# Both layers' weights of a chunk prepared together, sum buffers in 4 KB pieces, and three copies per pair, in a banded attention and FFN kernel

## The chip, the cores and the metric

One core of a Trainium2 chip. The metric is the device time of one execution in microseconds; a lower time is better. TensorE (PE) does matrix products, PEld is its weight load, VectorE is DVE, ScalarE is ACT, GpSimd is POOL, and SyncE (SP) issues the transfers (DMAs).

## The reference

```python
# q, k, v: (8, 8, 576, 64) float32;  w_in: (512, 2048), w_out: (2048, 512) float64
scores = q @ k.T / sqrt(64)                       # per batch and head
mask   = (rel >= 0) & (rel < 64)                  # rel = query position - key position
attn   = softmax(where(mask, scores, -1e9))
x      = (attn @ v) as 4608 tokens x 512
h      = x @ w_in
g      = where(h >= 1, h, where(h <= -1, 0, (h + 1)**2 / 4))
out    = g @ w_out                                # float32
```

## The kernel before

The 4608 tokens are nine tiles of 512. Each tile needs its attention (36 steps of 128 tokens in all) and then both FFN layers, taken in 16 chunks of 128 hidden features: chunk f has first-layer weights `wts[f, 0]` (L873 multiplies by them) and second-layer weights `wts[f, 1]` (L924). Weights and activations are each split into a high and a low part of float32r, and three products are summed.

**Weights.** They arrive as 64-bit floats and are turned into the two parts once, during tile 0: a load (`w_load`, L284), two ACT passes (`w_rest` L317, `w_sign` L294), three short DVE passes (L298, L298, L310), `w_join` (L321), `w_high` (ACT, L265) and `w_low` (DVE, L333). The first four chunks are done singly, layer by layer. From chunk 4 on the work is done in doubles: one double is one layer of the two chunks f and f+1, so the first layers of 4 and 5 come in one double and their second layers in another.

**Two ways of computing the first layer.** Tiles 0 and 1 (t < PLAIN) compute it plainly. Tiles 2 to 8 use a scheme with seven products per pair of chunks instead of eight (`ffn_products`, L824; the sums of the products are put together in `h` by L840). For it the kernel forms, during tile 1, for each of the eight pairs n of chunks, the seven operands of weights and keeps them in DRAM (`kept[n]`):
- `sum_pass` (L723) copies the three operands that are plain weights. Before, these are six copies per pair: three operands, for the high and the low part each.
- `sum_whole`, `sum_sums`, `sum_high`, `sum_low` (L734, L743, L265, L753) compute the four others on DVE, POOL and ACT in a buffer `half`, for the two halves c of a pair, and `sum_keep` (L758, L759) stores them. A pair's second half c=1 follows the first. For n < 2 the buffers are those of tile 0's activations (`xh0`, `xl0`), so that n=1 needs what n=0 has stored; later they lie in `TMP_SLOT` and `H_SLOT`.

During tiles 2 to 8, `ring_load` (L796) reads the kept operands of a pair back into two rings of two slots each. The rings, the tile's operands (`x_tiles`; `xs` in the trace) and `h` lie in space that held first-layer weights, which is free once tile 1 and the sums have used it.

**The order of the work** is written by a planner (`Plan`): each piece of work has a key, a cost per engine, pieces it comes after, and buffers it takes and gives back. The planner goes through planned time engine by engine, takes the piece with the lowest key among those that can start, and writes it down. What it writes is the program order of each engine and of SP's queue, and every engine works in that order. Its costs decide the order and nothing else: a piece that in truth takes longer than planned holds up what stands behind it. A DMA's planned cost is SP's time, plus a lag until what needs it can go on. Keys count steps; a tile of 512 tokens is 21.33 steps, so a chunk is 4/3 steps. The sums have the key `step(1) + S_PACE * n + S_LATE`.

The dependences between instructions are by region of a buffer, and waits are set for them whatever the planner assumes.

A gate (L897) is the step min/max that ends a chunk's activation; it frees the PSUM buffer `ps_h`, of which there are two.

Of the kernel before, what the change touches and what calls it, by code (L numbers as in the profile page):

```python
# [20 lines left out]
P = 128  # L21
# [19 lines left out]
W_LEAD = 0.57  # L41
W_PAIR = 0, 2.0
W_FIRST = (20.54, -1.96, 1.46, 0.57, -0.16)
# [7 lines left out]
W0_KEY = -100.2  # L51
FIRST_LOAD = 0, 1, 0
M_LATE = 1
W0_STEP = 11.75
FINE = 4
# [31 lines left out]
PLAIN = 2  # L87
S_LATE = 2
S_LATER = 2
S_PACE = 2  # L90
# [5 lines left out]
EARLY_2 = 1.5  # L96
IN_A = "w6_0", "w8_0"
IN_B = "w10_0", "w12_0"
H_SLOT = "w4_0"
TMP_SLOT = "w3_0"  # L100
# [93 lines left out]
def banded_attention_then_ffn(ctx: ExitStack, tc: tile.TileContext, q, k, v, w, masks, out, dims):  # L194
# [3 lines left out]
    NP = H // 2  # L198
    NF = 2 * w.shape[0]
    NB = S // QB  # L200
# [78 lines left out]
    def w_load(g, eng=nc.sync):  # L279
        f, nf, u = g  # L280
        m = nf * DM
        ws[g] = t = wpool.tile([P, 4 * m], U16, name="raw", tag=f"w{f}_{u}")
        src = w[f // 2, :, u, f % 2:f % 2 + nf].bitcast(U16)
        eng.dma_start(out=t[:, :4 * m - 1], in_=src.rearrange("p f n -> p (f n)")[:, 1:])  # L284

    def w_sign(g):

        m = g[1] * DM  # L290
# [21 lines left out]
    def w_rest(g):  # L312

        m = g[1] * DM
# [8 lines left out]
    def w_high(g, eng):  # L323
        f, nf, u = g
        ws[g] = t = wpool.tile([P, nf, 2, DM], F32R, name="wts", tag=f"w{f}_{u}")
        for j in range(nf):
            wts[f + j, u] = t[:, j]
        us[g] = us[g].bitcast(F32).rearrange("p (u n) -> p u n", n=DM)
        copy(eng, t[:, :, 0], us[g])
# [6 lines left out]

    def add_weights(f, nf, unit):
        g = f, nf, unit
        m = nf * DM
        act, high, join, low, small = 105 + .916 * m, 92 + .844 * m, 10 + 1.22 * m, 67 + 1.05 * m, 90 + .25 * m  # L340
        key = f * W_STEP - (W_FIRST[f] if f < len(W_FIRST) else W_LEAD) + (W_PAIR[unit] if nf == 2 else .5 * unit)
        x = add(W0_KEY + W0_STEP * (f + .5 * nf * unit), dict(SP=W_LOAD * nf), lambda e: None if g == FIRST_LOAD else w_load(g), lag=DMA_LAG)
# [8 lines left out]
        for j in range(nf):  # L351
            w_ready[f + j, unit] = x

# [144 lines left out]


    xfs, xops = {}, {}  # L500

# [6 lines left out]
    def x_tiles(t):  # L508
        if t in xops:
            return  # L510
        shape = [P, 2, 2, 2, 2 * SB]
        a, b = (xpool.tile(shape, F32R, name="xs", tag=f"{n}{t % 2}") for n in ("xh", "xl"))
        if t % 2:
            c = wpool.tile(shape, F32R, name="xs", tag="w14_0")
            rest = [c[:, 0], c[:, 1], wpool.tile(shape[:1] + shape[2:], F32R, name="xs", tag="w3_0")]
        else:
            rest = [wpool.tile(shape[:1] + shape[2:], F32R, name="xs", tag=f"w{f}_0") for f in range(3)]
        xops[t] = a, b, rest, [rest[0], a[:, 1], b[:, 0], a[:, 0], rest[1], b[:, 1], rest[2]]
# [200 lines left out]
    def sum_pass(n):  # L719
        f0, f1 = by_chunk(n)  # L720
        for part in range(2):
            for o, w_, e in (0, f0, 0), (5, f0, 1), (6, f1, 1):
                nc.sync.dma_start(out=kept[n][:, part, :, o], in_=w_[:, part, :, e].bitcast(F32))  # L723

    def sum_whole(n, c, i, eng):
        if i:
            pass
        elif n < 2:
            half_of[n, c] = [xpool.tile([P, 8, P], F32, name="half", tag=("xh0", "xl0")[c])]
        else:  # L730
            half_of[n, c] = [wpool.tile([P, 8, P], F32, name="half", tag=H_SLOT if n > 2 and c else TMP_SLOT)]
        t = half_of[n, c][0]
        w_ = by_chunk(n)[i]
        engine[eng].tensor_tensor(  # L734
            out=t[:, 2 * i:2 * i + 2], in0=w_[:, 0, c].bitcast(F32), in1=w_[:, 1, c].bitcast(F32), op=ALU.add
        )
# [26 lines left out]
    def add_sums(n):  # L763
        key = step(1) + S_PACE * n + (S_LATE if n < 2 else S_LATER)
        ready = [w_ready[2 * n, 0], w_ready[2 * n + 1, 0]]
        xp = add(key, dict(SP=1600), lambda e: sum_pass(n), ready + [x_in[0]], lag=DMA_LAG)
        reads, keeps = [xp], [xp]
        for c in range(2):
            after = ready + ([x_in[0]] if n < 2 else [l1[1, 3], *sums_read[1]]) + sum_last
            if n == 2 and c:  # L770
                after.append(keeps[-1])
            elif n == 3 and not c:
                after.append(sums_kept[2][-1])
            elif n > 2 and c:
                after += [l1[1, 4], l1[1, 5], *sums_read[2]]
            k = key + c * S_PACE / 2
# [8 lines left out]
            x = add(k, tt(4 * P), lambda e, c=c: sum_low(n, c, e), [xh], shared=True)  # L785
            x = add(k, dict(SP=1500), lambda e, c=c: sum_keep(n, c), [x], lag=DMA_LAG, gives=[("tmp", xs), ("o", xh)])
            keeps.append(x)
# [5 lines left out]
    def ring_load(t, n, i):  # L793
        rings[t, n, i] = r = wpool.tile([P, 2, 2, 4 - i, P], F32R, name="wr", tag=(IN_A, IN_B)[i][n % 2])
        for part in range(2):
            nc.sync.dma_start(out=r[:, part].bitcast(F32), in_=kept[n][:, part, :, R_OPS[i]])  # L796

    ring_last = [[], []]

    def add_ring(t, n, i, key):  # L800
        after = [*sums_kept[n], *ring_last[i]]
        if t == PLAIN and n < 2:
            m = int((IN_A, IN_B)[i][n % 2].split("_")[0][1:]) // 2
# [7 lines left out]
    prods, hs, hbox = {}, {}, []  # L811

    def ffn_products(t, n, i):
# [7 lines left out]
        for ps, c, o, k in todo:  # L821
            for j, (part, xp) in enumerate(((0, 0), (0, 1), (1, 0))):
                for cp in range(2):
                    nc.tensor.matmul(  # L824
                        ps[:, c * 2 * SB:(c + 1) * 2 * SB], lhsT=r[:, part, cp, o], rhs=xo[k][:, xp, cp],
                        start=i < 2 and c == 0 and j == 0 and cp == 0,
                        stop=(i == 2 or i == 3 and c == 1) and j == 2 and cp == 1, skip_group_check=True,
                    )

    def h_of(t, n):  # L830
        if not hbox:
            hbox.append(wpool.tile([P, 2, 4 * 2 * SB], F32, name="h", tag=H_SLOT))
        return hbox[0][:, n % 2]

# [151 lines left out]
    def add_ffn(t):  # L986
        first, before, x_out = {}, [x_in[t - 1]] if t else [], {}
        done, gates = None, []
        for q in range(NF):
            f = place(t, q)  # L990
            for r, key in parts(t, q):
# [36 lines left out]
                for i0 in subs(r) if by_sub else [None]:  # L1028
                    some = subs(r) if i0 is None else [i0]
                    xo = add(  # L1030
                        key + out_late(t, q, i0), dict(PE=3 * len(some) * 229), lambda e, f=f, r=r, i0=i0: ffn_out(t, f, r, i0),
                        [xl, w_ready[f, 1], *over], takes=[] if q else ["acc"] * len(some),
# [34 lines left out]
    for f in range(NF):  # L1067
        for unit in range(2):
            if f < FINE:
                add_weights(f, 1, unit)  # L1070
            elif f % 2 == 0:
                add_weights(f, 2, unit)
    for t in range(len(TILES)):
# [4 lines left out]
        if t + 1 == PLAIN:  # L1078
            for n in range(NF // 2):
                add_sums(n)  # L1080
            x_after[t + 1] = [l1[1, f] for f in range(3)] + sums_read[0] + sums_read[1] + sums_kept[0] + sums_kept[1]
            x_after[t + 2] = [l1[1, NF - 1], *sums_read[7], *sums_kept[7]]
# [59 lines left out]
```

## Time and profile before

| | |
|---|---|
| median of 3 runs | 906.59 us (905.62 to 907.96) |
| the profiled execution's own time | 907.99 us |
| its span, first to last instruction | 906.2 us |
| mean granted TensorE clock | 0.987 |
| SP's transfers of operands to DRAM | 48 plain copies of 128 KB, 32 stores of 256 KB |
| weight loads | 8 of 511.8 KB, 12 of 1023.8 KB |

The page gives busy shares by engine, then the span in 40 slices of 22.7 us, each digit a tenth of busy time (9 is 90% or more); the row of the granted clock has tenths of full speed. An answer for a stretch of time has the stretch, its length, then for each engine the busy us and the count of instructions, then the clock, the busy share of the 16 DMA engines and GB/s. In the order of time, a row has start and length in us, and in brackets the idle time ahead and what ended it. Tile 1's first products come at about 132.7 us, tile 2's at 254.8 us.

### The profile page before, as it was taken

The numbers are of one execution on the slowest core, as the hardware profiler recorded it, in microseconds if no ns is written. First come the engines' busy times: TensorE is split into PE (matmuls) and PEld (weight loads), VectorE is DVE, ScalarE is ACT, GpSimd is POOL, SyncE is SP. The second block draws the span as 40 slices with busy tenths as digits, with TensorE's granted clock in tenths as the row PEclk, the third lists the DMA queues.
The fourth block names the chain that finished last, engine by engine and source line by source line (L and its number), as shares of the span: only waits on it lengthen the run. The fifth ranks groups of instructions, "written<-read, shape, count | busy, mean of one in ns | idle before, by whom it ended". The sixth has DMA issues, their size and how long they took to land.

```text
span 906.2 us, 20363 instructions
## 1 busy us (share of the span) xinstructions
PE 875.5 (97%) x7839; PEld 762.9 (84%) x7839; DVE 656.1 (72%) x1391; ACT 506.8 (56%) x1291; POOL 264.2 (29%) x268
## 2 busy tenths in 40 slices
PE   7699997999799999999999999999999999999998
PEld 5587885887688888888898889888988888899997
DVE  6999996598977868777686767676767676833331
ACT  7998863554455555655565537454655565434343
POOL 1000034455432232423142324232413242322222
PEclk9999996999899999999999999999999999999999
DMA  9991149447567666766676658666765664557531
GB/s 333 410 377 55 54 146 291 146 157 239 198 214 226 213 199 215 253 204 193 218 251 216 216 181 285 204 204 216 260 208 194 206 228 163 164 169 237 175 117 47
DMA packets 108033, 187.60 MB, mean 207 GB/s; under 512 B 8480, under 2 KB 49696, under 8 KB 107936
## 3 DMA queue, kind: packets, MB, share of 16 engines
q1 hardware_dynamic: 107648, 185.38, 60.9%
q8 instruction: 62, 1.02, 0.5%
q10 hardware_dynamic: 288, 0.92, 0.3%
q14 instruction: 35, 0.29, 0.1%
HBM read 162.15 MB, written 24.12 MB: 206 GB/s over the span
## 4 chain that ended last, share of the span: by engine, by line
PE 75%; DVE 12%; DMA 5%; ACT 3%; issue 2%; SPq 2%; POOL 0%; ACTq 0%; DVEq 0%
PE acc L924 36%; PE ps_h L824 27%; PE ps_h L873 6%; DVE ptd L455 4%; PE ps_a L484 3%; PE ps_a L409 3%; DVE a L897 2%; DMA kept<-half 2%; DMA kt<-in_k 2%; SPq L723 1%; ACT a L885 1%; DVE h L840 1%; DVE sm L449 1%; DVE half L734 1%; DVE half L743 1%
## 5 line engine op out<-in xcount | busy, mean ns | idle before, releaser
L924 PE MATMUL acc<-wts,gh 128*128 128x512 f32 x1154 | 363.2, 396 | 2.7 <-ACT o L265 2.7
L824 PEld LDWEIGHTS ps_h<-xs,wr 128*128 128x128 f32 x2352 | 294.5, 189 | 10.3 <-DVE h L840 0.7
L824 PE MATMUL ps_h<-xs,wr 128*128 128x256 f32 x2352 | 299.2, 282 | 0.3 <-DVE h L840 0.3
L907 POOL TENSOR_TENSOR gl<-a,gh 128x512 fp32r<-128x512 f32 (+1 forms) x130 | 167.6, 1290 | 427.5 <-ACT gh L902 389.7
L924 PEld LDWEIGHTS acc<-wts,gh 128*128 128x128 f32 x1154 | 207.9, 189 | 44.6 <-ACT o L265 3.4
L924 PE MATMUL acc<-wts,gl 128*128 128x512 f32 x577 | 225.9, 391 | 0.0
L840 DVE TENSOR_TENSOR h<-h,ps_h 128x256 f32<-128x256 f32 x280 | 117.5, 420 | 127.8 <-PE ps_h L824 113.0
L902 ACT CAST gh<-a 128x512 fp32r<-128x512 f32 (+1 forms) x149 | 90.0, 604 | 133.9 <-PE acc L924 112.2
L455 DVE STREAM_TRANSPOSE ptd<-sm 32x256 f32<-32x256 f32 x336 | 146.5, 436 | 6.3
L924 PEld LDWEIGHTS acc<-wts,gl 128*128 128x128 f32 x577 | 108.7, 188 | 23.9
L885 ACT ACTIVATE a<-h 128x512 f32<-128x512 f32 x112 | 69.9, 624 | 72.3 <-DVE h L840 71.4
L897 DVE SCALAR_TENSOR_TENSOR a<-a,h 128x512 f32<-128x512 f32 x112 | 85.7, 765 | 27.7 <-ACT a L890 16.2
L873 PE MATMUL ps_h<-xh,wts 128*128 128x512 f32 (+1 forms) x296 | 93.3, 385 | 10.7 <-DVE a L897 6.6
L437 ACT ACTIVATE sm<-sm,nm 128x96 f32<-128x96 f32 (+1 forms) x256 | 93.0, 365 | 12.2 <-DVE nm L430 12.1
L890 ACT ACTIVATE a<-a 128x512 f32<-128x512 f32 (+1 forms) x139 | 85.8, 617 | 4.3
L873 PEld LDWEIGHTS ps_h<-xh,wts 128*128 128x128 f32 x296 | 56.8, 200 | 22.6 <-DVE a L897 8.1
L873 PE MATMUL ps_h<-xl,wts 128*128 128x512 f32 (+1 forms) x148 | 56.3, 380 | 0.7 <-DVE xl L497 0.6
L265 ACT COPY h<-ps_h 128x256 f32<-128x256 f32 x77 | 28.7, 372 | 47.3 <-PE ps_h L824 43.6
L549 POOL TENSOR_TENSOR xs<-u,xs 128x256 fp32r<-128x256 f32 (+1 forms) x45 | 42.3, 971 | 32.0 <-ACT xs L265 32.0
L734 POOL TENSOR_TENSOR half<-wts 128x256 f32<-128x256 f32 x12 | 9.4, 790 | 140.1 <-PE ps_h L873 123.7
L437 ACT ACTIVATION_READ_ACCUMULATOR sm<-sm,nm 128x1 f32 x256 | 47.9, 187 | 0.0
L484 PEld LDWEIGHTS ps_a<-ptd,vt 128*64 128x64 f32 x992 | 32.0, 137 | 13.1 <-DVE ptd L455 3.6
(89 smaller groups left out, 728.3 us busy)
## 6 DMA issues: line engine op xcount, KB each, us to landing
wr<-kept SPq DMA_DIRECT2D x112, 512.0 KB, 4.7
wr<-kept SPq DMA_DIRECT2D x112, 384.0 KB, 3.9
vt<-in_v SPq DMA_DIRECT2D x72, 256.0 KB, 4.9
kt<-in_k SPq DMA_DIRECT2D x35, 384.0 KB, 5.4
raw<-in_w SPq DMA_DIRECT2D x12, 1023.8 KB, 10.3
qt<-in_q SPq DMA_DIRECT2D x36, 256.0 KB, 4.8
out<-o SPq DMA_DIRECT2D x33, 256.0 KB, 4.0
kept<-wts SPq DMA_DIRECT2D x48, 128.0 KB, 2.4
```

The costliest lines, as they stand in the source:

```text
L437: nc.scalar.activation(sm[:, p, :], (ps if masked else sm)[:, p, :], AF.Exp, bias=nm[:, p:p + 1], scale=scale if masked else 1.0, accum_ou ...
L455: nc.vector.transpose(dst[:, :, r], src[:, :, c * SQ:(c + 1) * SQ])
L484: nc.tensor.matmul(ps[half[h], p, n], lhsT=vt[i][:, c:c + D], rhs=pt[h][:, p, n], start=True, stop=True)
L824: nc.tensor.matmul(ps[:, c * 2 * SB:(c + 1) * 2 * SB], lhsT=r[:, part, cp, o], rhs=xo[k][:, xp, cp], start=i < 2 and c == 0 and j == 0 and ...
L840: nc.vector.tensor_tensor(out=h[:, to:to + 256], in0=h[:, of:of + 256], in1=ps[:, at:at + 256], op=ALU.add)
L873: nc.tensor.matmul(ps, lhsT=wts[f, 0][:, part, c * P:(c + 1) * P], rhs=x[:, c, r], start=(c == 0 and j == 0), stop=(c == NP - 1 and j == 2),)
L885: nc.scalar.activation(gs[t, f, r.start][0], phs[t, f, r.start], AF.Relu, bias=0.5, scale=0.5)
L890: nc.scalar.activation(a, a, AF.Square)
L897: nc.vector.scalar_tensor_tensor(out=a, in0=a, scalar=1.0, in1=ps, op0=ALU.min, op1=ALU.max)
L902: nc.scalar.copy(g[1], g[0])
L907: engine[eng].tensor_tensor(out=g[2], in0=g[0], in1=g[1].bitcast(F32), op=ALU.subtract)
L924: nc.tensor.matmul(acc[t, i][:, n], lhsT=g[:, sub], rhs=wts[f, 1][:, part, n], start=(q == 0 and j == 0), stop=(q == NF - 1 and j == 2 and ...
```

## The change

1. **Weights.** From chunk 4 on a double is both layers of one chunk (`add_weights(f, (0, 1))`); the host lays the weights out to match, and the size and number of the loads stay. Keys: a double of chunk f has the key of the first layer of chunk f; before, the second layers of a pair came two steps after the first ones.
2. **Pieces.** The second-layer weights of a chunk now stand beside the first-layer weights in one 8 KB buffer, so the space that becomes free is the 4 KB half `piece(f)`. Operands of even tiles lie in the pieces of chunks 4, 5 and 2 (before: 0, 1, 2), of odd ones in 14, 15 and `TMP_SLOT`; the rings in pieces 6 to 13; `h` in the buffers of chunks 0 and 1 (before: 4 and 5), and with it the second halves of the later sums. The lists of what has to be over by then are changed to match.
3. **Copies.** `sum_pass` makes three copies per pair in place of six, each for both parts at once.
4. **Gates.** In tiles 0 and 1 a gate is no longer planned after the gate before it.
5. **Planner figures.** A pass costs SP 2000 ns in place of 1600, a store 750 in place of 1500; both have a lag of 2300 ns in place of 1300; the sums' keys are one step higher (S_LATE, S_LATER 2 to 3); a second-layer product of tiles 0 and 1 is planned at 232 ns in place of 229.

```diff
-FIRST_LOAD = 0, 1, 0
+FIRST_LOAD = 0, (0,)
-S_LATE = 2
-S_LATER = 2
+S_LATE = 3
+S_LATER = 3
-IN_A = "w6_0", "w8_0"
-IN_B = "w10_0", "w12_0"
-H_SLOT = "w4_0"
+X_PIECES = (4, 5, 2), (14, 15)
+R_PIECES = (6, 8), (10, 12)
+H_SLOT = "w0_0", "w1_0"
...
-    def add_weights(f, nf, unit):
-        g = f, nf, unit
-        m = nf * DM
+    def add_weights(f, units):
+        g = f, units
+        m = len(units) * DM
...
-        key = f * W_STEP - (...) + (W_PAIR[unit] if nf == 2 else .5 * unit)
+        key = f * W_STEP - (...) + .5 * units[0]
...
+    def piece(f):
+        return wts[f, 0].rearrange("p a n -> p (a n)")
...
     def sum_pass(n):
         f0, f1 = by_chunk(n)
-        for part in range(2):
-            for o, w_, e in (0, f0, 0), (5, f0, 1), (6, f1, 1):
-                nc.sync.dma_start(out=kept[n][:, part, :, o], in_=w_[:, part, :, e].bitcast(F32))
+        for o, w_, e in (0, f0, 0), (5, f0, 1), (6, f1, 1):
+            nc.sync.dma_start(
+                out=kept[n][:, :, :, o].rearrange("p a c n -> p (a c) n"),
+                in_=w_[:, :, :, e].bitcast(F32).rearrange("p a c n -> p (a c) n"),
+            )
...
-        xp = add(key, dict(SP=1600), lambda e: sum_pass(n), ready + [x_in[0]], lag=DMA_LAG)
+        xp = add(key, dict(SP=2000), lambda e: sum_pass(n), ready + [x_in[0]], lag=O_LAG_DMA)
...
-                after += [l1[1, 4], l1[1, 5], *sums_read[2]]
+                after += [l1[1, 0], *sums_read[0]]
...
-            x = add(k, dict(SP=1500), lambda e, c=c: sum_keep(n, c), [x], lag=DMA_LAG, ...)
+            x = add(k, dict(SP=750), lambda e, c=c: sum_keep(n, c), [x], lag=O_LAG_DMA, ...)
...
-            needs += [l1[1, 4], l1[1, 5], *sums_kept[NF // 2 - 1]]
+            needs += [l1[1, 0], l1[1, 1], *sums_read[0], *sums_kept[NF // 2 - 1]]
...
-                gates = [xg]
+                gates = [xg] if t >= PLAIN else []
...
-    for f in range(NF):
-        for unit in range(2):
-            if f < FINE:
-                add_weights(f, 1, unit)
-            elif f % 2 == 0:
-                add_weights(f, 2, unit)
+    for f in range(NF):
+        for units in ((0,), (1,)) if f < FINE else ((0, 1),):
+            add_weights(f, units)
...
-            x_after[t + 1] = [l1[1, f] for f in range(3)] + sums_read[0] + sums_read[1] + ...
+            x_after[t + 1] = [l1[1, f] for f in (2, 4, 5)] + sums_read[1] + sums_read[2] + ...
```

More of the change, by code (lines that the diff above doesn't have):

```diff
@@ L279, in w_load @@
     def w_load(g, eng=nc.sync):
-        f, nf, u = g
-        m = nf * DM
-        ws[g] = t = wpool.tile([P, 4 * m], U16, name="raw", tag=f"w{f}_{u}")
-        src = w[f // 2, :, u, f % 2:f % 2 + nf].bitcast(U16)
-        eng.dma_start(out=t[:, :4 * m - 1], in_=src.rearrange("p f n -> p (f n)")[:, 1:])
+        f, units = g
+        m = len(units) * DM
+        ws[g] = t = wpool.tile([P, 4 * m], U16, name="raw", tag=f"w{f}_{units[0]}")
+        src = w[f, :, units[0]:units[-1] + 1].bitcast(U16)
+        eng.dma_start(out=t[:, :4 * m - 1], in_=src.rearrange("p u n -> p (u n)")[:, 1:])
     def w_sign(g):
-        m = g[1] * DM
+        m = len(g[1]) * DM
         t = ws[g].bitcast(BF16)
@@ L323, in w_high @@
     def w_high(g, eng):
[L324 to L327, printed above, removed]
+        f, units = g
+        ws[g] = t = wpool.tile([P, len(units), 2, DM], F32R, name="wts", tag=f"w{f}_{units[0]}")
+        for j, u in enumerate(units):
+            wts[f, u] = t[:, j]
         us[g] = us[g].bitcast(F32).rearrange("p (u n) -> p u n", n=DM)
@@ L350, in add_weights @@
         x = add(key - W_LATE[6], dict(DVE=low), lambda e: w_low(g), [x], gives=[("u", xr)])
-        for j in range(nf):
-            w_ready[f + j, unit] = x
+        for u in units:
+            w_ready[f, u] = x
     xt = {}
@@ L512, in x_tiles @@
         a, b = (xpool.tile(shape, F32R, name="xs", tag=f"{n}{t % 2}") for n in ("xh", "xl"))
+        rest = [piece(f).rearrange("p (a c n) -> p a c n", a=2, c=2) for f in X_PIECES[t % 2]]
         if t % 2:
[L514 to L517, printed above, removed]
+            rest.append(wpool.tile(shape[:1] + shape[2:], F32R, name="xs", tag=TMP_SLOT))
         xops[t] = a, b, rest, [rest[0], a[:, 1], b[:, 0], a[:, 0], rest[1], b[:, 1], rest[2]]
@@ L730, in sum_whole @@
         else:
-            half_of[n, c] = [wpool.tile([P, 8, P], F32, name="half", tag=H_SLOT if n > 2 and c else TMP_SLOT)]
+            half_of[n, c] = [wpool.tile([P, 8, P], F32, name="half", tag=H_SLOT[0] if n > 2 and c else TMP_SLOT)]
         t = half_of[n, c][0]
@@ L785, in add_sums @@
             x = add(k, tt(4 * P), lambda e, c=c: sum_low(n, c, e), [xh], shared=True)
-            x = add(k, dict(SP=1500), lambda e, c=c: sum_keep(n, c), [x], lag=DMA_LAG, gives=[("tmp", xs), ("o", xh)])
+            x = add(k, dict(SP=750), lambda e, c=c: sum_keep(n, c), [x], lag=O_LAG_DMA, gives=[("tmp", xs), ("o", xh)])
             keeps.append(x)
@@ L793, in ring_load @@
     def ring_load(t, n, i):
-        rings[t, n, i] = r = wpool.tile([P, 2, 2, 4 - i, P], F32R, name="wr", tag=(IN_A, IN_B)[i][n % 2])
+        rings[t, n, i] = r = []
         for part in range(2):
-            nc.sync.dma_start(out=r[:, part].bitcast(F32), in_=kept[n][:, part, :, R_OPS[i]])
+            m = 4 - i
+            r.append(piece(R_PIECES[i][n % 2] + part)[:, :2 * m * P].rearrange("p (c o n) -> p c o n", c=2, o=m))
+            nc.sync.dma_start(out=r[part].bitcast(F32), in_=kept[n][:, part, :, R_OPS[i]])
     ring_last = [[], []]
@@ L830, in h_of @@
     def h_of(t, n):
-        if not hbox:
-            hbox.append(wpool.tile([P, 2, 4 * 2 * SB], F32, name="h", tag=H_SLOT))
-        return hbox[0][:, n % 2]
+        if len(hbox) == n and n < 2:
+            hbox.append(wpool.tile([P, 4 * 2 * SB], F32, name="h", tag=H_SLOT[n]))
+        return hbox[n % 2]
     def h_copy(t, n, to, eng):
@@ L1080, in banded_attention_then_ffn @@
                 add_sums(n)
-            x_after[t + 1] = [l1[1, f] for f in range(3)] + sums_read[0] + sums_read[1] + sums_kept[0] + sums_kept[1]
+            x_after[t + 1] = [l1[1, f] for f in (2, 4, 5)] + sums_read[1] + sums_read[2] + sums_kept[0] + sums_kept[1]
             x_after[t + 2] = [l1[1, NF - 1], *sums_read[7], *sums_kept[7]]
```

24 lines of the change are left out of this document (11 added, 13 removed).

## The prediction

> **What bounds the kernel now.** I read the page's share table and slices first: is one engine full, and where is it not?
>
> ```profile
> PE 875.5 (97%) x7839; PEld 762.9 (84%) x7839; DVE 656.1 (72%) x1391; ACT 506.8 (56%) x1291; POOL 264.2 (29%) x268
> ...
> PE   7699997999799999999999999999999999999998
> PEclk9999996999899999999999999999999999999999
> DMA  9991149447567666766676658666765664557531
> ```
>
> PE bounds it, but slices 6 and 10 (from 136 and 227 us) show fewer busy tenths and a lower granted clock together. So I cut the span at those places and read busy time, clock and DMA share of each stretch (columns: length, then busy us of PE, PEld, DVE, ACT, POOL; clock, DMA share, GB/s).
>
> ```profile
> 0.00:50.00 50.00, 36.98 (x438) 30.93 (x439) 41.81 (x108) 41.72 (x120) 2.91 (x16) 0.97 0.98 375
> ...
> 140.00:160.00 20.00, 13.95 (x73) 11.07 (x68) 11.81 (x24) 8.04 (x28) 10.42 (x15) 0.66 1.00 313
> 160.00:227.00 67.00, 66.62 (x607) 53.24 (x605) 51.77 (x107) 35.96 (x96) 36.03 (x45) 1.00 0.52 178
> 227.00:246.00 19.00, 14.30 (x135) 11.22 (x136) 18.43 (x43) 9.03 (x28) 9.88 (x14) 0.82 0.60 212
> 246.00:890.00 644.00, 641.13 (x5858) 573.08 (x5857) 443.17 (x949) 333.59 (x862) 192.68 (x165) 1.00 0.63 205
> ```
>
> From 246 us on PE is idle 2.9 us in 644: tiles 2 to 8 hold nothing for this change. Three places do: the start (13.0 us idle), "stall 1" (140 to 160) and "stall 2" (227 to 246). Stall 1: idle 20 - 13.95 = 6.05 us; a mean clock of 0.66 means about 13.6 us at half clock, of which some 3.4 were idle (the second and third gap below), so 10.2 us of matmuls took twice their time and lost 5.1. Together 11.1 us. Stall 2 the same way: idle 4.7, and 6.8 us at half clock less 0.9 idle, so 3.0 lost; 7.7 us.
>
> Next the order of time (start, length, engine, line; in brackets the idle time before, and what ended it), of PE, SP's queue, POOL, DVE and ACT; here and below single rows are picked out of it.
>
> ```profile
> 139.56 1.15 PE L484 MATMUL ps_a<-ptd,vt 128*64 128x64 f32 x32
> 143.32 0.58 PE L873 MATMUL ps_h<-xh,wts 128*128 128x256 f32 x1 [2.60 <-DVE xh L267]
> 150.69 1.22 PE L924 MATMUL acc<-wts,gh 128*128 128x512 f32 x2 [2.65 <-ACT o L265]
> 152.99 0.58 PE L873 MATMUL ps_h<-xh,wts 128*128 128x256 f32 x1 [0.65 <-DVE a L897]
> 122.47 14.10 SPq L723 DMA_DIRECT2D kept<-wts  x24
> 137.21 0.40 SPq L759 DMA_DIRECT2D kept<-half  x1
> 147.47 0.38 SPq L759 DMA_DIRECT2D kept<-half  x1
> 131.95 1.29 POOL L753 TENSOR_TENSOR half<-half,o 128x512 fp32r<-128x512 f32 x1
> 141.64 0.42 DVE L734 TENSOR_TENSOR half<-wts 128x256 f32<-128x256 f32 x1 [1.78 <-DMA kept<-half]
> 150.70 0.99 DVE L734 TENSOR_TENSOR half<-wts 128x256 f32<-128x256 f32 x1 [4.55 <-DMA kept<-half]
> 150.05 0.58 ACT L265 COPY o<-acc 128x512 f32<-128x512 f32 x1 [7.19 <-DMA kept<-o]
> ```
>
> All three gaps hang on one queue. SP spends 14.10 us on 24 plain copies (`sum_pass`). The first finished sum was complete at 133.2 (POOL L753), but its store stands behind those copies and is issued at 137.21; its landing shows where DVE's L734, which needs that buffer again, can start: 141.64. DVE works in order, so the cast `xh`, for which PE waits, stands behind it. The second store goes out at 147.47 behind 12 more copies; DVE (4.55 us) and ACT (7.19 us) wait for it, ACT holding back the copy that frees PE's `acc`. The chain of waits for 118 to 165 us says the same:
>
> ```profile
> by line: PE ps_h L873 25.5%; SPq L723 24.8%; PE acc L924 11.7%; DVE ptd L464 7.0%; DMA kept<-half 6.7%; issue 4.7%; DVE a L897 3.7%; DVE gl L907 2.3%; PE ps_a L484 2.3%; DVE half L734 2.1%; SPq L758 1.9%; DVE ptd L455 1.7%; ACT a L890 1.4%;
> ```
>
> **The change, part by part.** *Copies.* 48 become 24 of twice the bytes, with the same 512-byte pieces. What does one cost?
>
> ```profile
> L723 SPq DMA_DIRECT2D kept<-wts x48: 382/486/2125, 122.5 to 156.9; - x48
> q1 hardware_dynamic: 4101, 1.98, 82.7%
> kept<-wts SPq DMA_DIRECT2D x48, 128.0 KB, 2.4
> ```
>
> The first row gives the issue (minimum, median, maximum ns); the second is the DMA view of 128 to 136 us: 4101 packets kept the 16 engines 82.7% busy, so one packet takes 0.827 x 8 x 16 / 4101 us = 25.8 ns, and a doubled copy of 512 packets 0.83 us. The 12 copies that replace the 24 ahead of the first store therefore take at best 12 x 0.486 = 5.8 us (issue alone), 9.9 us if the engines' time decides, and 14.1 us if issuing scales with the packets. I take 9.9: during those copies the engines were 83% busy already, so they are the nearest limit. Then SP is free at 132.4 and the first store leaves when its sum is ready, about 133.5, which is 3.7 us earlier; it lands near 138, before DVE asks at 139.9. Ahead of the second store 36 copies become 18: 14.9 us, and about 2 us for the store and two loads between them, so it leaves near 139.5, 8 us earlier, and lands near 143, before DVE and ACT ask (146.2 and 142.9). Of stall 1 there stays what PE waits for by itself: it ends L484 at 140.7 and needs one cast of 0.7 us, so about 1 us, too little to leave a half-clock stretch. **Stall 1: -10.0 us**; the ends are -11.1 (all of it) and 0 (14.1 us for 12 copies).
>
> The clock price is where a page speaks differently. The Trainium skill (TensorE: Matmul & The Clock Gate, Part 1) says half rate follows at least one idle window of about 3.4 us; here the 2.60 us gap was already followed by matmuls at half clock. By the page a remainder of up to 2.6 us would cost only itself; by the row it could add half of a 3.4 us stretch, 1.7 us, and the sum would read -8.3 in place of -10.0 where such a gap stays.
>
> *Planner figures.* A pass is planned at 2.0 us in place of 1.6 (six copies measured 14.10/4 = 3.5), a store at 0.75 + 2.3 in place of 1.5 + 1.3 us. They move no time themselves, only the order. The sums' keys come one step later, S_LATE 2 to 3; a chunk is 4/3 steps and 2.78 + 2.77 us of PE (first two rows), so a step is 4.2 us. Fewer gates stand behind sums on DVE, but the last sum comes later. This bears on stall 2:
>
> ```profile
> 76.80 2.78 PE ps_h L873 x12
> 79.58 2.77 PE acc L924 x12
> 217.20 0.76 DVE L734 TENSOR_TENSOR half<-wts 128x256 f32<-128x256 f32 x2 [3.36 <-DMA kept<-half]
> 239.74 0.79 PE L873 MATMUL ps_h<-xh,wts 128*128 128x512 f32 x1 [3.90 <-DVE a L897]
> 246.35 0.32 SPq L759 DMA_DIRECT2D kept<-half  x1
> 254.79 3.73 PE L824 MATMUL ps_h<-xs,wr 128*128 128x256 f32 x30
> ```
>
> There PE waits for a gate that DVE reaches late: DVE lost 3.36 us at 217 to a store that left among ring loads, not plain copies, and was then full (18.43 of 19 us). From 140 to 246 DVE does 11.81 + 51.77 + 18.43 = 82 us; in a tile 10 us shorter that is 82 of 96, so the crowd stays. **Stall 2: 0**, between -7.7 (gone) and +4.2 (the last sum a step late, all of it on PE's path).
>
> *Weights.* The number, size and prices of the 12 double loads and their preparations stay. Before, two first layers were prepared, then two second layers; now both layers of one chunk. The k-th double is ready as before, but chunk 6 needs the third, where it needed the second:
>
> ```profile
> 55.73 1.24 DVE L333 TENSOR_TENSOR wts<-u,wts 128x1024 fp32r<-128x1024 f32 x1
> 67.08 1.22 DVE L333 TENSOR_TENSOR wts<-u,wts 128x1024 fp32r<-128x1024 f32 x1
> 66.56 0.47 PE L873 MATMUL ps_h<-xh,wts 128*128 128x512 f32 x1
> 69.44 0.63 PE L924 MATMUL acc<-wts,gh 128*128 128x512 f32 x2
> ```
>
> PE starts chunk 6 at 66.56; the third double ends at 68.30, 1.7 us later. In return the second layer of chunk 4, used at 69.44, is ready over 11 us sooner (with the first double), but its gate is not. **Weights: +0.9 us**, the middle of 0 (attention matmuls fill the gap) and +1.7.
>
> *Gates in free order.* 37 gates of tiles 0 and 1 lose a planned order; no instruction goes. One gap of the start ends with a gate:
>
> ```profile
> 30.00:40.00 10.00, 7.06 (x74) 6.52 (x74) 9.68 (x24) 9.31 (x20) 0.00 (x0) 1.00 1.00 419
> 38.53 0.39 PE L873 MATMUL ps_h<-xh,wts 128*128 128x256 f32 x1 [2.08 <-DVE a L897]
> ```
>
> DVE is busy 9.68 of 10 us there, so a reorder only swaps work: **0**, between -2.1 and +2.1 (as much lost by a swap the other way).
>
> *Buffers.* Operands of tile 2 lie in the first-layer weights of chunks 4, 5, 2 (before 0, 1, 2), `h` in those of 0 and 1, the later sums' halves in 0.
>
> ```profile
> 180.64 0.32 SPq L759 DMA_DIRECT2D kept<-half  x1
> 234.41 1.53 ACT L265 CAST xs<-u 128x512 fp32r<-128x512 f32 x4
> ```
>
> The operands are written from 234 us; the sums of chunks 4 and 5 (the sixth half, first row) are 53 us past by then, and their matmuls longer; halves are free earlier than before. **0**; without that cover a write would wait for the third pair's sums. The pieces are halves of tiles whose other half PE reads all the time, but no instruction is added for it, and 644 us of steady work should repeat.
>
> Sum: -10.0 + 0 + 0.9 + 0 = -9.1 us. The profiled execution took 907.99 (span 906.2), 1.4 above the median of 906.59; from the median the forecast is **897.5 us**.
>
> **The rivals.** *The DMA engines take the queue's place.* The Trainium skill (DMA: Bandwidth & Descriptors, "Queues, rings and completion order") says each engine consumes descriptors in ring order; by it a store issued early still waits for the packets ahead. Merging removes no packet, and from 140 to 160 us the DMA share was 1.00 with loads and stores between the copies. If SP runs ahead and five or six pairs are queued before the first store, 18 x 0.83 = 14.9 us stand before it, more than today's 14.10, and stall 1 stays but for one gap of about 2.6 us: 904 us. Against it: SP cannot run past a store whose sum isn't ready, and the planned 2.0 us put only three or four pairs before it.
>
> *Both stalls go.* If DVE no longer loses its 3.36 us and gates come before the sums: 11.1 + 7.7 less 0.9 gives 888.7 us. For it: later sum keys; against: DVE's 82 us.
>
> *The sums become the bound (slower).* The last store went at 246.35 and the first product of tile 2 at 254.79, and `h` of tile 2 takes the buffer of the last half. If the series of sums doesn't move with PE (its period is set by two buffers and their stores) and starts each a step later, PE arrives early, and waits until 4.2 us after today's start: 906.6 + 4.2 = 910.8 us. It decides as soon as the last store leaves later than about 250 us.
>
> **How the numbers follow.** Forecast 0.55 (its own range 892 to 902); both stalls gone 0.18; DMA engines 0.15; sums as the bound 0.12. The range from 886.5 (both gone, and the start's gate gap too) to 905.5 leaves out the slower case and a part of the third. A run can tell 0.3%, 2.7 us: faster takes 0.55 + 0.18 + three fifths of the third = 0.82; same the rest of it and a little of the slower = 0.08; slower 0.10.
>
> **What would show it.** Right: L723 x24 on SP at 0.5 to 0.9 us each, the first kept<-half before 135 us, no DVE or ACT wait for kept over 1 us before 160 us, granted clock 1.00 there. Wrong: a 10 us hole in PE near 145 us with SP idle (engines), kept<-half landing over 5 us after its issue, a PE wait for the last sum ahead of the first L824, or a gap before chunk 6 over 2 us.

## The result, and the profile after

The changed kernel takes **892.68 us** (median of 4 runs, 890.89 to 893.97) where the kernel before takes 906.88 (905.62 to 907.96): a ratio of **0.9843, with a 95% interval of 0.9821 to 0.9864**. That is 14.2 us off; the forecast was 9.1 off, 897.5, with a range of 886.5 to 905.5. The profiled execution of the changed kernel took 890.89 us (span 889.1, mean clock 0.994).

First the shares, slices and stretches of the changed kernel, read as those of before:

```profile
PE 869.5 (98%) x7839; PEld 758.8 (85%) x7839; DVE 650.4 (73%) x1384; ACT 508.0 (57%) x1292; POOL 268.8 (30%) x274
...
PE   7899999999999999999999999999999999999998
PEclk8999999999999999999999999999999999999999
```

```profile
0.00:50.00 50.00, 39.98 (x446) 33.80 (x447) 40.27 (x105) 40.93 (x119) 2.93 (x16) 0.90 0.95 359
...
140.00:160.00 20.00, 19.84 (x184) 16.65 (x185) 14.46 (x32) 11.27 (x31) 10.97 (x14) 1.00 1.00 335
227.00:246.00 19.00, 18.20 (x183) 15.02 (x182) 17.69 (x38) 11.89 (x43) 11.79 (x15) 1.00 0.69 240
```

The two slices of 7 tenths, at 136 and 227 us, are gone. Stall 1 keeps 0.16 of its 6.05 idle us. Stall 2 keeps little, and from 50 to 860 us there is no half clock at all. In the first 50 us PE is idle 10.0 us instead of 13.0, but this execution ran 10.2 us of them at half clock, and the profiled one of the kernel before 3.4. In order of time, rows of PE and SP:

```profile
140.16 0.73 PE L928 MATMUL acc<-wts,gh 128*128 128x512 f32 x2 [0.50 <-DVE o L266]
223.34 0.50 PE L877 MATMUL ps_h<-xh,wts 128*128 128x512 f32 x1 [1.42 <-DVE a L901]
248.95 1.03 PE L483 MATMUL ps_a<-ptd,vt 128*64 128x64 f32 x28 [0.95 <-DVE ptd L454]
123.29 9.31 SPq L722 DMA_DIRECT2D kept<-wts  x12
135.14 0.33 SPq L761 DMA_DIRECT2D kept<-half  x1
151.49 0.40 SPq L761 DMA_DIRECT2D kept<-half  x1
237.11 0.38 SPq L761 DMA_DIRECT2D kept<-half  x1
```

Twelve double copies hold SP for 9.31 us (24 single ones 14.10), and the first `half` is stored at 135.14, where it was 137.21. The second goes out *later* than before (151.49 for 147.47), yet no PE gap hangs on it: DVE now does the casts of `xh` (at 138.82) and `xl` and its gates up to 150.4 ahead of the sum that needs this store, and starts that sum at 155.18. Before, sums that waited for a store stood in front of both (L734 at 141.64 and 150.70). Who waited for these transfers from 115 to 165 us (us, times):

```profile
L722 SPq DMA_DIRECT2D kept<-wts x24: 517/660/1215, 123.3 to 150.0; - x24
...
  DVE half L736: 4.8, 1
  POOL half L736: 2.5, 1
```

### The profile page after: what moved, and what is told of

Read it like the earlier page. It is cut to its first block, busy times and chain, and to the rows that moved or that the text cites. A ratio compares the mean times of both kernels' runs of the same rounds, so it can differ in the third digit from the quotient of the medians.

```text
span 889.1 us, 20426 instructions
## 1 busy us (share of the span) xinstructions
PE 869.5 (98%) x7839; PEld 758.8 (85%) x7839; DVE 650.4 (73%) x1384; ACT 508.0 (57%) x1292; POOL 268.8 (30%) x274
## 4 chain that ended last, share of the span: by engine, by line
PE 76%; DVE 15%; ACT 4%; DMA 2%; issue 2%; POOL 1%; SPq 0%; ACTq 0%; DVEq 0%; POOLq 0%
PE acc L928 36%; PE ps_h L828 28%; DVE ptd L454 5%; PE ps_h L877 4%; PE ps_a L483 3%; PE ps_a L408 3%; DVE a L901 2%; ACT sm L436 2%; DVE sm L448 1%; DVE h L844 1%; ACT a L889 1%; DMA vt<-in_v 1%; DMA raw<-in_w 1%; ACT a L894 1%; DVE sm L425 1%
## 5 line engine op out<-in xcount | busy, mean ns | idle before, releaser
L828 PE MATMUL ps_h<-xs,wts 128*128 128x256 f32 x1488 | 195.9, 282 | 0.1
L828 PEld LDWEIGHTS ps_h<-xs,wts 128*128 128x128 f32 x1488 | 184.8, 189 | 1.7 <-DVE h L844 0.6
L828 PEld LDWEIGHTS ps_h<-wts 128*128 128x128 f32 x864 | 119.6, 189 | 8.7 <-DVE h L844 0.2
L828 PE MATMUL ps_h<-wts 128*128 128x256 f32 x864 | 125.9, 282 | 0.0
L877 PE MATMUL ps_h<-xh,wts 128*128 128x512 f32 (+1 forms) x296 | 89.6, 372 | 3.8 <-DVE a L901 2.3
L877 PEld LDWEIGHTS ps_h<-xh,wts 128*128 128x128 f32 x296 | 54.2, 191 | 14.8 <-DVE a L901 3.2
L877 PE MATMUL ps_h<-xl,wts 128*128 128x512 f32 (+1 forms) x148 | 54.5, 368 | 0.5 <-DVE xl L496 0.5
L736 POOL TENSOR_TENSOR half<-wts 128x256 f32<-128x256 f32 x17 | 13.3, 799 | 127.0 <-PE ps_h L877 124.5
## 6 DMA issues: line engine op xcount, KB each, us to landing
raw<-in_w SPq DMA_DIRECT2D x12, 1023.8 KB, 10.3
```

Source lines behind the costliest of these rows:

```text
L828: nc.tensor.matmul(ps[:, c * 2 * SB:(c + 1) * 2 * SB], lhsT=r[part][:, cp, o], rhs=xo[k][:, xp, cp], start=i < 2 and c == 0 and j == 0 and ...
L877: nc.tensor.matmul(ps, lhsT=wts[f, 0][:, part, c * P:(c + 1) * P], rhs=x[:, c, r], start=(c == 0 and j == 0), stop=(c == NP - 1 and j == 2),)
```

## The experiments

Parts were added to the kernel before one at a time, and taken out of the changed kernel one at a time. Each ratio goes by the kernel before, measured beside it (medians of 906.45 to 907.20 us). The intervals are about 0.2% to either side; by two such intervals put together, an estimate, two kernels less than some 2.5 us apart are not told apart.

| kernel | median us | ratio to before (95%) |
|---|---|---|
| three copies alone | 899.86 | 0.992 (0.9901 to 0.9938) |
| free gates alone | 899.44 | 0.9918 (0.9902 to 0.9935) |
| gates and copies | 896.2 | 0.9884 (0.987 to 0.9899) |
| gates, copies, planner figures | 892.53 | 0.9846 (0.9823 to 0.987) |
| **changed kernel** | **892.68** | **0.9843 (0.9821 to 0.9864)** |
| changed, six copies | 897.71 | 0.99 (0.988 to 0.992) |
| changed, six copies on two queues | 893.34 | 0.9854 (0.9833 to 0.9876) |
| changed, weights by layer | 893.43 | 0.9854 (0.9831 to 0.9878) |
| changed, gates in order | 899.85 | 0.9914 (0.9895 to 0.9933) |
| changed, sums' key 2 | 895.08 | 0.9866 (0.9847 to 0.9885) |
| changed, queue figures of before | 893.58 | 0.9857 (0.9833 to 0.988) |
| changed, key 2 and queue figures of before | 898.27 | 0.9902 (0.9886 to 0.9917) |
| changed, sums' key 4 | 899.07 | 0.9919 (0.9898 to 0.994) |

To see where each gains, I summed PE's busy time weighted with the granted clock, from the matmul and clock records, up to three times (us of work done):

| kernel | by 110 us | by 165 us | by 270 us |
|---|---|---|---|
| before | 95.3 | 139.2 | 235.9 |
| three copies alone | 92.9 | 144.0 | 242.6 |
| free gates alone | 99.2 | 153.4 | 247.3 |
| gates and copies | 96.1 | 151.1 | 247.0 |
| gates, copies, figures | 97.4 | 151.0 | 252.8 |
| changed | 95.6 | 150.1 | 251.8 |
| changed, six copies | 95.7 | 147.6 | 244.4 |
| changed, sums' key 2 | 96.3 | 150.8 | 248.1 |
| changed, queue figures of before | 95.9 | 149.7 | 249.5 |
| changed, key 2 and queue figures of before | 96.1 | 150.3 | 244.6 |

The first column is unsteady: the first two kernels have the same program there, but the start of one profiled execution had 3.4 us at half clock and that of the other 10.2. Differences between columns are steadier. They still belong to single executions: the two profiled ones of the kernel before and the changed one lie 17.1 us apart (spans of 906.2 and 889.1), the medians 14.2.

### Three copies alone

The kernel before with `sum_pass` of the changed one; the orders of PE, DVE, ACT and POOL stay.

```diff
-        for part in range(2):
-            for o, w_, e in ...:                       # six copies
+        for o, w_, e in ...:                           # three, both parts each
```

> The kernel before with three copies per pair and nothing else; the order of work on PE, DVE, ACT and POOL is the one of before, instruction by instruction. Theory (SP's queue): the first two stores of sums leave some 4 and 8 us earlier, stall 1 falls from 11.1 us to about 1, stall 2 and the start stay: 896 to 898 us, ratio near 0.989. Rival (the order): the gain came from where the planner put things, so this kernel stays within 3 us of before, 904 to 908. Rival (DMA engines): the stores leave earlier but land as late, because the packets are the same: 903 to 907, with kept<-half landing over 5 us after its issue.

899.86 us, 7.0 less: the theory's way, but short of its 896 to 898. A stretch and rows of PE, SP and DVE:

```profile
140.00:160.00 20.00, 17.82 (x182) 13.95 (x183) 14.27 (x30) 11.40 (x33) 12.07 (x18) 0.91 0.88 296
```

```profile
142.81 0.38 PE L873 MATMUL ps_h<-xh,wts 128*128 128x256 f32 x1 [1.28 <-DVE xh L267]
143.54 0.39 PE L873 MATMUL ps_h<-xl,wts 128*128 128x256 f32 x1 [0.34 <-DVE xl L497]
231.41 0.79 PE L873 MATMUL ps_h<-xh,wts 128*128 128x512 f32 x1 [3.38 <-DVE a L897]
123.28 9.71 SPq L723 DMA_DIRECT2D kept<-wts  x12
134.11 0.33 SPq L759 DMA_DIRECT2D kept<-half  x1
142.22 0.50 SPq L759 DMA_DIRECT2D kept<-half  x1
207.83 0.76 DVE L734 TENSOR_TENSOR half<-wts 128x256 f32<-128x256 f32 x2 [1.75 <-DMA kept<-half]
```

The queue does what the prediction said (9.71 us for 9.9, first store at 134.11 for 133.5). But from 140 to 160 us 2.18 us stay idle, and the first two gaps are followed by 3.4 us at half clock (0.91 over the stretch, which loses 1.8 us). Of the 11.1 us of stall 1 that leaves a gain of 7.1, which is what the median shows. Stall 2 is still there: DVE loses 1.75 us to a store at 207 us and then comes late with a gate.

### Six copies in the changed kernel

The same lines the other way round; again the four engines' orders stay.

> The changed kernel with six copies per pair again; its order on PE, DVE, ACT and POOL is unchanged. Theory (SP's queue): 12 copies become 24 of about 0.58 us in front of the first store, which goes from 133.8 to about 138 us; a wait of DVE for kept<-half of 4 to 9 us and a hole in PE near 142 us return: 898 to 904 us, 5 to 11 above the changed kernel. Rival (the order): the changed order with its longer planned passes already keeps the stores clear of the copies, and the time stays within 3 us of 892.7.

897.71 us, 5.0 more, at the lower edge of the theory. SP, PE's largest gap near stall 1, and who waited for `kept` from 115 to 165 us:

```profile
123.14 15.52 SPq L723 DMA_DIRECT2D kept<-wts  x24
139.28 0.40 SPq L761 DMA_DIRECT2D kept<-half  x1
141.72 0.73 PE L928 MATMUL acc<-wts,gh 128*128 128x512 f32 x2 [2.21 <-DVE o L266]
```

```profile
  DVE half L736: 8.9, 1
  POOL half L736: 8.0, 2
```

The waits come back (8.9 and 8.0 us for 4.8 and 2.5), and PE's gap at 142 us is 2.21 us where the changed kernel has 0.50. By the table, 2.5 us of work are lost by 165 us and 4.9 more by 270, so much of the price is paid behind stall 1. The copies are worth 7.0 us on the old order and 5.0 on the new.

### Six copies on two queues

Is it SP's queue, or the size of the transfers at the DMA engines? Here the packets stay those of six copies, and the second part is issued by ScalarE.

```diff
-                nc.sync.dma_start(out=kept[n][:, part, :, o], ...)
+                (nc.sync, nc.scalar)[part].dma_start(out=kept[n][:, part, :, o], ...)
```

> The changed kernel with six copies per pair, three of them issued from SP's queue and three from ScalarE's, at the planned place of the step; the order of all other instructions is that of the changed kernel. Theory A (six copies cost their issue time on one queue: 15.5 us for the first 24, where 12 large ones take 9.3): SP's half of the first 24 is issued in about 8 to 10 us, and most of the 5 us that six copies cost on one queue come back: 892 to 895 us. Theory B (smaller transfers cost by themselves, at the DMA engines): the stores leave as late as with six copies on one queue and the time stays at 897 to 898 us. Theory C (ScalarE, which issues 24 transfers of some 0.4 us, is delayed in front of the second layer): 898 us or more.

893.34 us: 4.4 of the 5.0 us are back (theory A). SP is done after 7.34 us:

```profile
123.06 7.34 SPq L723 DMA_DIRECT2D kept<-wts  x12
135.82 0.33 SPq L761 DMA_DIRECT2D kept<-half  x1
128.02 1.47 ACTq L723 DMA_DIRECT2D kept<-wts  x3
```

So the cost was the copies' time on one queue, which issues in order, and neither the bytes nor the size of a copy. With two queues fewer packets also stand ahead of the store on its own queue, but that isn't where the gain is: the store lands 4.0 us after its issue here, and 2.4 us with six copies on one queue. It gains by leaving 3.5 us earlier (135.82 for 139.28).

### Weights by layer in the changed kernel

`add_weights`, `FIRST_LOAD` and the host's layout as before, everything else as changed.

> The changed kernel with the weights prepared as before (two first layers, then two second layers of a pair), all else as changed. Theory: the start's 1.9 us (first product of tile 1 at 130.8 in place of 132.7 us) came from preparing both layers of a chunk together, so the time rises by about 2 us to 894 to 895 us. Rival: the order of the weights is worth nothing (PE is full from 50 us on) and the 1.9 us came from the gates: 892 to 893.5 us. Rival (my term +0.9): it falls by 0.9 us to 891 to 892.

893.43 us, not told apart from 892.68 (the first rival). The weights' new order is worth nothing that shows.

### Gates in order in the changed kernel

```diff
-                gates = [xg] if t >= PLAIN else []
+                gates = [xg]
```

> The changed kernel with the gates of tiles 0 and 1 in a row again. Theory: gates are worth nothing by themselves, 892 to 893.5 us, with the first product of tile 1 near 130.8 us. Rival: the start's 1.9 us are theirs, and this time rises to 894.5 or more, with PE's gap before the second half of chunk 1 (0.92 us at 40.4) back at 2 us. Since the planner writes a new order, up to 2 us either way may be reshuffling.

899.85 us: 7.2 more, so the forecast's zero falls. Gaps come back in both places, the start (there also 2.08 us for a gate at 39.15) and stall 2, and stall 1 stays closed:

```profile
42.87 1.98 PE L408 MATMUL ps_a<-kt,qt 64*64 64x128 f32 x32 [2.04 <-DMA kt<-in_k]
238.93 0.80 PE L928 MATMUL acc<-wts,gl 128*128 128x512 f32 x1 [5.58 <-POOL gl L911]
```

### Free gates alone

The kernel before with that one line changed.

> The kernel before with only the gates of tiles 0 and 1 taken out of their chain; six copies per pair, weights by layer and all buffers stay. The orders of all engines are planned anew. Theory A (the free gates are worth about 7 us by themselves: the 2.08 us hole at 38.53 and the wait for in_k behind it go from the start, 2 to 4 us, and the new order also closes the hole of 230 to 246 us, 4 to 6 us): 898 to 902 us, stall 1 at 140 to 160 us still there at about 11 us. Theory B (chaining the gates again in the changed kernel cost 7 us because the new order happened to leave a 5.58 us hole at 239 us; freed alone they give the start only): 903 to 905 us, with a hole of 3 us or more and half clock between 225 and 250 us. Theory C (the forecast's zero): 906 to 908 us.

899.44 us, 7.0 less. Theory A had the size and missed the place: stall 1 goes, with six copies per pair, and a hole stays later. Around the gap at 38 us, DVE and PE, first before and then with free gates:

```profile
37.26 0.69 DVE L333 TENSOR_TENSOR wts<-u,wts 128x512 fp32r<-128x512 f32 x1
38.06 0.41 DVE L897 SCALAR_TENSOR_TENSOR a<-a,ps_h 128x256 f32<-128x256 f32 x1
42.51 1.10 PE L409 MATMUL ps_a<-kt,qt 64*64 64x128 f32 x32 [2.30 <-DMA kt<-in_k]
```

```profile
35.14 0.41 DVE L897 SCALAR_TENSOR_TENSOR a<-a,ps_h 128x256 f32<-128x256 f32 x1
38.12 0.41 DVE L897 SCALAR_TENSOR_TENSOR a<-a,ps_h 128x256 f32<-128x256 f32 x1
38.59 0.39 PE L873 MATMUL ps_h<-xh,wts 128*128 128x256 f32 x1 [0.44 <-DVE a L897]
43.03 1.10 PE L409 MATMUL ps_a<-kt,qt 64*64 64x128 f32 x32
137.17 0.69 DVE L267 CAST xh<-ps_a 128x512 fp32r<-128x512 f32 x1
116.29 17.80 SPq L723 DMA_DIRECT2D kept<-wts  x30
212.43 0.51 PE L873 MATMUL ps_h<-xh,wts 128*128 128x512 f32 x1 [2.30 <-DVE a L897]
236.05 0.80 PE L924 MATMUL acc<-wts,gl 128*128 128x512 f32 x1 [3.56 <-POOL gl L907]
```

A gate that stood behind weights on DVE until 38.06 has its counterpart at 35.14. It frees a `ps_h` sooner; PE has other matmuls to do, and reaches the attention step at 43.03, when `kt` is there: both gaps, 2.08 and 2.30 us, shrink to 0.44. By 110 us that is 3.9 us of work more at the same clock. Further on stall 1 doesn't form either. In the new order SP begins the copies at 116.29, 6.2 us earlier, and on DVE the cast `xh` (137.17) no longer stands behind a sum that waits for a store. The second store leaves at 152.11, later than before, and DVE waits 6.0 us for it up to 156.04, but no PE gap hangs on that. How much of the gain is owed to the copies' start and how much to DVE's order is not separated.

### Gates and copies

Both edits on the kernel before; four engines as with free gates alone.

> The kernel before with the free gates and the three copies, nothing else; PE, DVE, ACT and POOL keep exactly the order of the kernel with the free gates alone. Theory A (these two parts carry the whole gain, and add): 891 to 895 us, the time of the changed kernel; against the free gates alone 7 us less, no half clock between 120 and 250 us. Theory B (they do not carry it all: the pieces of 4 KB and the later key of the sums are needed for stall 2): 896 to 899 us with a hole of 3 us or more between 225 and 250 us.

896.2 us. Theory B's time held; its hole of 3 us or more is two smaller ones (2.38 and 2.08 us). Had the two added, it would be 892.5; they overlap by some 3.7 us, since each alone removes most of stall 1 (from 110 to 165 us 51.1 and 54.2 us of work, both together 55.0, before 43.9). What is missing to the changed kernel lies between 165 and 270 us: 95.9 us of work done there, where the changed kernel does 101.7.

```profile
212.24 0.50 PE L873 MATMUL ps_h<-xh,wts 128*128 128x512 f32 x1 [2.38 <-DVE a L897]
235.55 0.50 PE L924 MATMUL acc<-wts,gl 128*128 128x512 f32 x1 [2.08 <-POOL gl L907]
```

### Gates, copies and planner figures, without pieces and weights

```diff
-S_LATE = 2
-S_LATER = 2
+S_LATE = 3
+S_LATER = 3
-        ... dict(SP=1600), lambda e: sum_pass(n), ..., lag=DMA_LAG)
+        ... dict(SP=2000), lambda e: sum_pass(n), ..., lag=O_LAG_DMA)
-            ... dict(SP=1500), lambda e, c=c: sum_keep(n, c), ..., lag=DMA_LAG, ...)
+            ... dict(SP=750), lambda e, c=c: sum_keep(n, c), ..., lag=O_LAG_DMA, ...)
```

> The kernel before with the free gates, the three copies and the changed planner's figures for the sums (key of 3 steps, 2000 and 750 ns of SP's queue, lag of 2300 ns); weights by layer and the old buffers stay. Theory A (weights and pieces of 4 KB are worth nothing; gates, copies and figures make the whole gain): 891 to 895 us, no hole over 2.5 us between 120 and 275 us. Theory B (the pieces are what let the planner close stall 2; the figures help only with them): 896 to 898 us as with gates and copies alone, with a hole of 2 us or more near 212 and 235 us.

892.53 us: the whole gain. Pieces and weights are not needed for it; theory A held, and 101.8 us of work are done from 165 to 270.

### Which of the figures

The changed kernel with the key at 2; with the queue figures of before; with both.

> The changed kernel with the sums' key at 2 steps as before in place of 3, all else as changed. Theory A (the key is no term of the gain): 891 to 895 us, no hole over 2.5 us after 120 us. Theory B (the sums coming one step later is what closed stall 2): 896 to 900 us, with a hole of 3 us or more and half clock between 200 and 250 us.

> The changed kernel with only the queue figures of before for the sums (1600 and 1500 ns of SP, lag of 1300 ns), the key at 3 steps as changed. With the key at 2 steps and these figures the time was 898.3 us, with the key at 2 and the changed figures 895.1. Theory A (key and figures add): about 896 us, 894.5 to 897. Theory B (the key decides alone, the figures only matter with the early key): 891 to 894 us. Theory C (the figures decide alone): 897 to 899 us, with a hole of 4 us or more between 210 and 250 us.

> The changed kernel with the planner's figures of before for the sums: key of 2 steps, 1600 and 1500 ns of SP's queue and the long lag for the copies and the stores. The three copies, the gates, the weights and the buffers are as changed. Theory A (the figures are no term): 891 to 895 us. Theory B (the figures carry the part of the gain that the copies alone, 7 us on the order of before, leave over): 897 to 901 us with a hole between 225 and 250 us, as in the kernel with three copies alone.

895.08, 893.58 and 898.27 us (the lag of before is the shorter one, 1300 for 2300 ns; the last text has it wrong). By the medians the key alone is worth 2.4 us, at the edge of what can be told, the queue figures alone 0.9, which is not told from none, and both together 5.6. The traces say more. With the key at 2 alone the hole of stall 2 is back, 3.4 us at half clock follow it, and from 165 to 270 us 97.3 us of work are done instead of 101.7; so theory B had the mechanism, and its time is missed by 0.9 us:

```profile
227.79 0.79 PE L877 MATMUL ps_h<-xh,wts 128*128 128x512 f32 x1 [4.70 <-DVE a L901]
```

With the queue figures of before alone (key 3) no gap there is over 1.1 us. With both, the hole is longer:

```profile
216.57 1.08 DVE L736 TENSOR_TENSOR half<-wts 128x256 f32<-128x256 f32 x1 [1.70 <-DMA kept<-half]
...
225.42 0.68 DVE L549 TENSOR_TENSOR xs<-u,xs 128x512 fp32r<-128x512 f32 x1
226.02 0.68 DVE L755 TENSOR_TENSOR half<-half,o 128x512 fp32r<-128x512 f32 x1
...
228.48 0.64 DVE L901 SCALAR_TENSOR_TENSOR a<-a,ps_h 128x512 f32<-128x512 f32 x1
...
229.17 0.79 PE L877 MATMUL ps_h<-xh,wts 128*128 128x512 f32 x1 [5.46 <-DVE a L901]
```

DVE loses 1.70 us to a store, and then sums and operands of tile 2 stand before the gate for which PE waits. With the key at 2 alone the same crowd stands before that gate (it starts at 227.10), with no such loss to a store. So it is the crowd, set by the key, that makes the hole, and the queue figures change its length.

### A later key still

`S_LATE` and `S_LATER` at 4, a try at a faster version.

> The changed kernel with the sums' key at 4 steps in place of 3, all else as changed; a try at a faster version. Theory A (2 steps cost 2.4 us over 3; later sums leave VectorE free around 225 us, and what is left of stall 2 there, 1.42 and 0.95 us, goes too): 889 to 892 us. Theory B (the sums then come too late for the rings that read them from tile 2 on, and the holes move behind 240 us): 893 to 898 us.

899.07 us, 6.4 more: theory B's way, and 1.1 us beyond its range:

```profile
244.63 0.79 PE L928 MATMUL acc<-wts,gl 128*128 128x512 f32 x1 [3.45 <-POOL gl L911]
245.84 0.32 SPq L761 DMA_DIRECT2D kept<-half  x1
```

The last store moves from 237.11 to 245.84 us, and the hole behind 240. But theory B's reason isn't seen: PE waits there for POOL's `gl`, which starts at 243.31 behind sums on POOL, and not for a read of the kept operands. Of the three keys tried, 3 is the fastest; over 2 it is so by no more than can just be told.

## Why the prediction was right or wrong

**Bound.** Right: from tile 2's first product to the end it is 651.4 us before and 649.6 after (from 254.79 and 239.49 us), so nearly all that changed lies ahead of it.

**Stall 1, -10.0 us.** The place came out as forecast: from 110 to 165 us the changed kernel does 54.5 us of work, the one before 43.9, 10.6 more. That the size agrees so well is in part luck, because the cause was only partly the copies. Alone they gave 7.0: the issue time of the first copies was right, but the second store left at 142.22, not 139.5, and "too little to leave a half-clock stretch" failed: two gaps of 1.28 and 0.34 us were followed by 3.4 us at half clock. Of the prediction's two sums for this term, the -8.3 that counts such a stretch is the nearer. By the Trainium skill (TensorE: Matmul & The Clock Gate, Part 1) half rate follows at least one idle window of about 3.4 us, so gaps this short would not lead to it; these runs disagree. In the changed kernel the second store did not leave 8 us earlier but 4.0 us later, and the sign "no DVE or ACT wait for kept over 1 us" failed (DVE waits 4.8 us): there it is the order on DVE that keeps PE from waiting, which the prediction did not have.

**Gates, 0.** The step that failed most. "A reorder only swaps work" counted DVE's load (9.68 of 10 us) and not what waits for which instruction. Weights that nobody awaited yet stood before a gate that PE awaited; swapping them cost next to nothing (the weights' pass of 37.26 starts at 37.32 with free gates). It also looked at the 2.08 us gap alone, and not at the 2.30 us wait for `kt` behind it, nor at the order after 110 us. Mis-sized: 0, between -2.1 and +2.1, where taking the part out of the changed kernel costs 7.2 and adding it to the one before gains 7.0.

**Stall 2, 0.** The same fault. "82 of 96, so the crowd stays": the crowd did stay, and the stall went.

```profile
140.00:239.00 99.00, 96.65 (x917) 77.63 (x918) 85.81 (x186) 56.57 (x163) 57.13 (x74) 1.00 0.66 222
```

In the changed kernel DVE is busy 85.81 of 99 us, and PE 96.65. From 165 to 270 us 5.0 us were gained, and by the runs on key and queue figures it is these that decide: with the key at 2 alone, 4.4 of them are gone. The bounds (-7.7 to +4.2) held.

**Weights, +0.9, and buffers, 0.** Within what can be told, both together are nothing (892.53 us without them); for the weights that is the lower bound.

**The sum.** It missed 5.1 us of 14.2: a term that was too large (copies) and two set at zero (gates, stall 2) on loads that were full. The terms also weren't independent: copies and gates alone make 7.0 each and together 10.3. The forecast of 897.5 is near the result because an excess on one term covers a part of what the zeros left out.

**The rivals.** *Both stalls go* (888.7) is nearest to what happened by mechanism; 1.42 and 0.95 us of stall 2 stay. *The DMA engines* did become busier, from 124 to 133 us, before and then after (packets, MB, and the packets' own times added up as a share of the 16 engines' time, which can pass 100%):

```profile
q1 hardware_dynamic: 4261, 2.16, 79.7%
```

```profile
q1 hardware_dynamic: 5480, 3.05, 109.9%
```

But the sign of this rival, a store that lands over 5 us after its issue, is not seen where stall 1 would have formed: the first two stores of `half` take 3.6 us each in the changed kernel and 3.8 and 3.9 with three copies alone, where they took 4.3 and 3.1 before. Only the third takes 5.2 us in the changed kernel, and PE does not wait for it. *The sums as the bound*: at key 3 the last store leaves before tile 2's first product (239.5 us) and the two moved together; at key 4 the kernel lost 6.4 us.

## What to carry to other kernels

Where engines work in program order, a full engine does not mean that reordering it is worth nothing: ask of each gap which instruction ended it, and what stood before that one that nobody was waiting for. Count a transfer's issue time on its queue; moving half of the issues to a second queue, with a look at when the transfers behind them land, tells the queue's cost from that of the bytes. Parts that act on the same stall don't add, so run them alone and together before a gain is credited to either, and count a planner's figures as a part of the change.

## What the runs showed of the hardware

- Half clock came in whole steps of 3.41 us (3.41, 6.83, 10.24, 13.65), and in each of the 14 profiled executions all its edges lie on one grid of such steps (before, those at 13.52, 143.22 and 238.80 us are 38 and 28 steps apart).
- Taken between 50 and 860 us and step by step of that grid, what preceded half clock is PE's idle time within one step at full clock: all nine steps with 1.88 us or more were followed by it, none with 1.48 us or less; of the three between, 1.62 us (three copies alone, 1.28 and 0.34 us) and 1.65 us (six copies, 1.03 and 0.62 us) were, and 1.73 us (gates and copies, at 234 us) was not. So short gaps in one step add up, and a gap that an edge divides counts in two parts: 2.30 us (free gates alone) fell into parts of 1.23 and 1.07 us and was not followed, 2.38 us (gates and copies) had 2.31 us in one step and was. That the limit lies near half a step is an estimate from these steps; why 1.73 us was not followed stays open.
- Before and with three copies alone, the program of the first 110 us is the same, and the profiled executions had 3.4 and 10.2 us at half clock in it, 2.4 us of work apart: a difference of that size between two profiles need not be the effect of an edit.
- Copies of twice the bytes landed 3.7 us after their issue (median), those of before 2.4, with the 16 engines full (340 GB/s for 241 from 124 to 133 us).
